# Attention products in fewer groups, other PSUM homes, and a first weight load in halves: a change to a fused linear-attention and feed-forward kernel

## The chip, the cores and the metric

The kernel runs on one core of a Trainium2 chip. The metric is the device time of one execution in microseconds (us): 514.23 us before, the median of three runs (513.65 to 514.88). The engines are TensorE (PE in the rows; PEld is its weight load), VectorE (DVE), ScalarE (ACT), GpSimd (POOL) and SyncE (SP), which here issues all the DMA transfers.

## The reference

```python
def _attn_ref(r, k, v, w, u) -> np.ndarray:      # 4 batches, 8 heads, 768 steps, head size 48
    for t in range(S):
        kt, vt, rt = (k[:, :, t], v[:, :, t], r[:, :, t])
        cur = np.einsum('bhd,bhe->bhde', u[None] * kt, vt)
        y[:, :, t] = np.einsum('bhd,bhde->bhe', rt, state + cur)
        state = w[None, :, :, None] * state + np.einsum('bhd,bhe->bhde', kt, vt)

def _moe_ref(x, w_in, w_out) -> np.ndarray:      # 3072 tokens, 384 -> 2048 -> 384
    h = x @ w_in
    sp = np.maximum(h, 0.0) + np.log1p(np.exp(-np.abs(h)))
    g = h * erf(sp)
    return (g @ w_out).astype(np.float32)
```

The attention's output, laid out as 3072 tokens of 384 features, is the `x` of the feed-forward. The weights `w_in` and `w_out` arrive as 64-bit floats.

## The kernel before, in words

**Attention.** The 768 steps are cut into six spans of 128, so that with four batches there are 24 chunks, numbered `g` = 0 to 23; four chunks (one span, all batches) make one of six blocks of 512 tokens. For a chunk the kernel scales r and k by powers of the decay (`R`, `K`), multiplies them on TensorE (`A`), masks the product and puts the u-term on its diagonal (`Q`, `M`, `P`), multiplies it with v and the state with r (`Y`, tile `y`), and multiplies k with v (`D`, tile `ds`), which VectorE adds to the state `sbd` (`S`). The result y is split into a rounded part and a residue (`X`), tile `x`.

**Feed-forward.** The work is 96 pairs (block, slice of 128 hidden features), numbered `n`. `f1(n)` (token `f`) is nine matmuls into a PSUM tile `h`: three slices of the input, times high part by high part, high by residue and low by high. Nine element-wise steps make the activation of `h`: `a`, `b`, `c`, `d`, `e`, `h` on ScalarE, `z`, `g` and `l` on VectorE. `h` rounds (tile `gh`) and `l` takes the residue (`gl`). `f2(n)` (token `p`) is nine matmuls of `gh`, `gl` with the output weights into three PSUM tiles `acc`.

**Weights.** `F` loads one of eight groups of 768 columns of `w_in` (F00 to F07) or `w_out` (F10 to F17); the steps `C..a` to `C..f` turn the 64-bit words into a 32-bit value and split it in a high and a low part (`wih`, `wil`, `woh`, `wol`). Group 00 serves the first two slices. There are two raw tiles and one tile `wt` for the value in the making.

**Order.** The string `ORDER` lists every step as a token, and each engine executes its instructions in the order in which the tokens stand there; a `+` at a token's end moves it to GpSimd, a `*` to ScalarE. `W2` is two matmuls on a tile of zeros, which produce nothing. What may wait is only the semaphores: an instruction waits for its operands and for its output's buffer, and everything behind it on its engine waits too.

**PSUM.** Of eight banks, three are the `acc` (pool `ps1`), two belong to `psa` and three to `ps3`. Before, the three of `ps3` hold, once the first four chunks are through, only the `h` tiles, in turn; the two of `psa` hold the A, y and ds of all later chunks. An `h` is read by `act_a`, `act_z`, `act_g`, `act_h` and `act_l`, and `act_g` writes its result back into it (lines 443, 449 and 454), so its bank is free only after `act_l`.

Of the kernel before, what the change touches and what calls it, by code (L numbers as in the profile page):

```python
# [706 lines left out]
P51 Q6c f3 c2 c1 d2 e2 Y4 D4 W2 C10e X4a d1 C10f C02a N5 X4b C02b C02c S4a C02d Y5 W2 p0x p0y p0z L7a F11 F03 L7b e1
a3 X5a b3 C02e R7+ C02f+ X5b g1 S4b h1 M60* M61+ A6 g2 z3 l1 C11a c3 d3 h2 e3 P60 C11b C11c C11d P61 f4 C11e a4 D5 Y6
p1 Q7a+ C11f+ b4 S5b g3 l2 X6a C03a f5 p2 K7+ z4 S5a X6b C03b L8a F12 C03c Q7b N7+ C03d Q7c N6+ M70+ M71+ A7 c4 h3 d4
e4 l3 g4 a5 C03e h4 b5 C03f f6 l4 z5 C12a c5 C12b C12c C12d L8b F14 F13 d5 a6 b6 z6 P70 e5 P71 g5 f7 C12e a7 p3 Y7  # L710
C12f+ Q8a b7 c6 z7 h5 d6 l5 e6 X7a c7 d7 e7 Q8b+ Q8c g6 X7b K8+ M80+ M81+ g7 p4 p5 f8 h6 l6 C13a C13b h7 C13c C13d l7
a8 b8 z8 C13e f9 f10 c8 a9 d8 b9 z9 S4d+ C13f+ R8+ e8 C14a F05 g8 C14b C14c p6 c9 a10 d9 h8 C14d l8 p7x p7y p7z A8 e9
C14e b10 O70a O70b F04 g9 O71a h9 f11 C14f+ P80 z10 l9 C05a a11 c10 b11 C05b P81 d10 O72a e10 z11 C05c g10 C05d p8x
p8y f12 D6 D7 p8z O71b L9a L9b F15 O72b L10a p9 c11 a12 d11 h10 l10 e11 g11 C05e C05f b12 z12 h11 l11 f13 p10 f14 p11
C04a c12 a13 d12 b13 e12 C04b C04c C04d F07 z13 g12 C04e c13 h12 l12 d13 S6a K10+ C04f+ a14 e13 g13 b14 z14 h13 l13
S7a f15 f16 C07a c14 p12 Q9a C07b C07c C07d a15 d14 b15 z15 e14 F06 g14 a16 C07e b16 z16 h14 l14 c15 C07f+ d15 e15 g15
S5d p13 f17 p14 C15a h15 c16 a17 d16 e16 b17 C15b l15 C15c C15d g16 F16 L10b z17 S7b p15x C15e h16 l16 p15y f18 f19
p15z c17 O150a d17 S7c+ S5c+ C15f+ S4c+ Y8 Q9b N8 S6b D8 p16x C06a a18 b18 e17 C06b C06c C06d g17 O151a a19 b19 z19
h17 l17 O150b z18 Q9c O152a c19 p16y p16z O152b F17 L11a L11b O230a O151b O231a p17 C06e d19 e19 c18 S8b C06f f20
Q10a+ g19 d18 h19 l19 e18 R10+ S8d+ Q10b+ C16a g18 h18 C16b l18 a20 f21 f22 b20 z20 a21 c20 d20 b21 e20 p18 C16c C16d  # L720
S8a Q11a g20 Q10c z21 a22 C16e h20 l20 b22 z22 c21 d21 c22 d22 e22 N9+ M90+ R9+ C16f+ g22 p19 f23 e21 h22 a23 g21 l22
# [112 lines left out]
```

## Time and profile before

| what | value |
|---|---|
| median of three runs | 514.23 us |
| the profiled execution's own time | 513.87 us |
| its span in the trace | 511.8 us |
| TensorE busy | 496.6 us, 97% |
| VectorE busy | 357.4 us, 70% |
| ScalarE busy | 390.4 us, 76% |
| GpSimd busy | 135.7 us, 27% |
| granted TensorE clock | 0.997 of full |

The span is the time from the first to the last recorded instruction; about 2 us of the execution lie outside it. An engine's busy time is the time in which at least one of its instructions ran. A row of the timeline gives the start in us, the length in us, the engine, the line of the kernel, the operation, the output and inputs by the program's names, and how many like instructions follow each other; matmuls overlap, so what one costs is read from start to start.

### The profile page before, as it was taken

How to read it: one execution, taken by the hardware profiler on the slowest of the kernel's cores; microseconds unless marked ns; L12 is line 12 of the kernel's file. 1: busy time of each engine (PE TensorE's matmuls, PEld its weight loads, DVE VectorE, ACT ScalarE, POOL GpSimd, SP SyncE). 2: the span in 40 equal slices, each digit the busy share in tenths (PEclk: the TensorE clock that was granted, in tenths of full speed). 3: DMA queues.
4: the chain of work that ended last, by engine and by line, in shares of the span. 5: the costliest groups of instructions: out<-in, count | busy, mean ns of one | idle time of the engine just before them, and what ended most of it. 6: DMA issues, size and time to landing. Idle time of an engine off the chain costs nothing.

```text
span 511.8 us, 11055 instructions
## 1 busy us (share of the span) xinstructions
PE 496.6 (97%) x4476; PEld 391.8 (77%) x4476; DVE 357.4 (70%) x642; ACT 390.4 (76%) x712; POOL 135.7 (27%) x135
## 2 busy tenths in 40 slices
PE   8798899999999999999999999999999999999995
PEld 4666677788877777787787787888777878777884
DVE  7999997888879878777755755676746555445542
ACT  2688888999887666776777867777878678878892
POOL 4564564133542044016001610226032100000000
PEclk9999999999999999999999999999999999999998
DMA  7953631754601072301006102214030000100001
GB/s 276 363 195 119 249 125 62 243 176 153 224 12 42 2 260 96 131 20 73 2 1 215 49 1 86 97 36 167 22 131 1 1 2 3 41 22 0 0 1 67
DMA packets 13993, 48.16 MB, mean 94 GB/s; under 512 B 1776, under 2 KB 2160, under 8 KB 13936
## 3 DMA queue, kind: packets, MB, share of 16 engines
q1 hardware_dynamic: 13936, 47.39, 26.4%
q8 instruction: 37, 0.61, 0.5%
q14 instruction: 20, 0.16, 0.1%
HBM read 41.09 MB, written 6.29 MB: 93 GB/s over the span
## 4 chain that ended last, share of the span: by engine, by line
PE 85%; DVE 5%; DMA 4%; ACT 3%; SPq 1%; issue 1%; ACTq 0%
PE acc L471 38%; PE h L411 37%; PE y L330 6%; PE A L301 3%; DMA out_dram<-o 2%; DMA raw<-in_win_dram 1%; PE ds L353 1%; DMA att<-in_att_dram 1%; DVE wt L130 1%; DVE wt L127 1%; DVE am L309 1%; DVE gl L454 1%; ACT s L435 0%; SPq L72 0%; ACT s L422 0%
## 5 line engine op out<-in xcount | busy, mean ns | idle before, releaser
L411 PE MATMUL h<-x,wih 128*128 128x512 f32 x576 | 184.8, 402 | 1.0 <-DVE gl L454 0.9
L411 PEld LDWEIGHTS h<-x,wih 128*128 128x128 f32 x576 | 106.4, 188 | 29.3 <-DVE gl L454 3.2
L471 PE MATMUL acc<-gh,woh 128*128 128x512 f32 x288 | 116.0, 403 | 0.0
L411 PE MATMUL h<-x,wil 128*128 128x512 f32 x288 | 114.3, 397 | 0.0
L471 PE MATMUL acc<-gh,wol 128*128 128x512 f32 x288 | 114.2, 397 | 0.0
L471 PE MATMUL acc<-gl,woh 128*128 128x512 f32 x288 | 114.1, 396 | 0.0
L427 DVE SCALAR_TENSOR_TENSOR s<-s,h 128x512 f32<-128x512 f32 x96 | 65.2, 683 | 46.8 <-ACT s L422 46.2
L454 DVE TENSOR_TENSOR gl<-h,gh 128x512 fp32r<-128x512 f32 x96 | 66.0, 689 | 39.8 <-ACT gh L449 38.3
L443 DVE SCALAR_TENSOR_TENSOR h<-s,h 128x512 f32<-128x512 f32 x96 | 66.0, 691 | 37.9 <-ACT s L439 37.3
L449 ACT CAST gh<-h 128x512 fp32r<-128x512 f32 x96 | 55.8, 582 | 36.1 <-DVE h L443 20.6
L418 ACT ACTIVATE s<-h 128x512 f32<-128x512 f32 x96 | 56.9, 593 | 27.5 <-PE h L411 27.1
L431 ACT ACTIVATE s<-s 128x512 f32<-128x512 f32 x96 | 60.0, 627 | 22.7 <-DVE s L427 22.4
L471 PEld LDWEIGHTS acc<-gh,woh 128*128 128x128 f32 x288 | 54.2, 188 | 14.2 <-issue 0.8
L411 PEld LDWEIGHTS h<-x,wil 128*128 128x128 f32 x288 | 54.3, 188 | 13.3 <-DVE wil L135 0.3
L471 PEld LDWEIGHTS acc<-gh,wol 128*128 128x128 f32 x288 | 54.3, 188 | 13.1
L471 PEld LDWEIGHTS acc<-gl,woh 128*128 128x128 f32 x288 | 54.3, 189 | 12.5
L422 ACT ACTIVATE s<-s 128x512 f32<-128x512 f32 x96 | 60.4, 630 | 1.7
L435 ACT ACTIVATE s<-s 128x512 f32<-128x512 f32 x96 | 60.4, 630 | 1.7
L439 ACT ACTIVATE s<-s 128x512 f32<-128x512 f32 x96 | 60.1, 629 | 1.7
L283 POOL TENSOR_TENSOR am<-idents,q 128x512 f32<-128x512 f32 x25 | 28.5, 1150 | 76.6 <-PE y L330 65.5
L309 DVE COPY_PREDICATED am<-mask,A 64x128 f32<-64x128 uint32 (+2 forms) x108 | 38.3, 389 | 3.0 <-PE A L301 1.9
L222 POOL TENSOR_TENSOR att<-att,wr 112x512 f32<-112x512 f32 x16 | 21.8, 1363 | 42.8 <-DMA att<-in_att_dram 42.8
(89 smaller groups left out, 467.5 us busy)
## 6 DMA issues: line engine op xcount, KB each, us to landing
att<-in_att_dram SPq DMA_DIRECT2D x22, 608.0 KB, 5.9
att<-in_att_dram SPq DMA_DIRECT2D x24, 512.0 KB, 4.0
raw<-in_win_dram SPq DMA_DIRECT2D x8, 768.0 KB, 4.7
raw<-in_wout_dram SPq DMA_DIRECT2D x8, 768.0 KB, 4.6
out_dram<-o SPq DMA_DIRECT2D x18, 256.0 KB, 2.6
part<-o SPq DMA_DIRECT2D x6, 256.0 KB, 4.8
o<-part SPq DMA_DIRECT2D x6, 256.0 KB, 3.0
att<-in_att_dram SPq DMA_DIRECT2D x2, 224.0 KB, 6.6
```

The lines of the kernel that those rows point to most:

```text
L309: nc.vector.copy_predicated(out=o, data=ap[rows, n, :, i], mask=mask[rows, n, None, i].to_broadcast(list(o.shape)).bitcast(U32))
L411: nc.tensor.matmul(out=h, lhsT=w[:, f, q, :], rhs=x[:, xi, q, :], start=k == 0, stop=k == 8)
L418: nc.scalar.activation(out=s1, in_=e["h"], func=AF.Tanh, bias=FB0, scale=FA0)
L422: nc.scalar.activation(out=s1, in_=s1, func=AF.Tanh, bias=FB1, scale=FA1)
L427: nc.vector.scalar_tensor_tensor(out=e["s"], in0=e["s1"], scalar=FG, in1=e["h"], op0=ALU.mult, op1=ALU.add)
L431: nc.scalar.activation(out=s, in_=s, func=AF.Tanh, bias=FB2, scale=FA2)
L435: nc.scalar.activation(out=s, in_=s, func=AF.Square, bias=FB3, scale=FA3)
L439: nc.scalar.activation(out=s, in_=s, func=AF.Square, bias=FB4, scale=FA4)
L443: nc.vector.scalar_tensor_tensor(out=h, in0=ff[n]["s"], scalar=FC, in1=h, op0=ALU.subtract, op1=ALU.mult, reverse0=True)
L449: nc.scalar.copy(out=e["gh"], in_=e["h"])
L454: eng.tensor_tensor(out=e["gl"], in0=e["h"], in1=e["gh"].bitcast(F32), op=ALU.subtract)
L471: nc.tensor.matmul(out=acc[e], lhsT=w[:, f, es], rhs=g, start=first and i == 0, stop=last and i == 2)
```

## The change

It does four things. The tiles y and ds of all chunks from the fourth on take their banks from `ps3`, where the `h` are; only the A stay in `psa`. The step `act_g` writes its result into the SBUF tile `s` instead of back into `h`, and `act_h` and `act_l` read it there. The first group of input weights is loaded and converted in two halves of 384 columns, with tokens `F00`, `C00.` and `F08`, `C08.`, in one raw tile and one `wt`. And the whole order is another one: 1,747 tokens instead of 1,739, some steps on other engines.

```diff
+    halves = {int(x[1]) for x in ORDER.split() if x[0] == "F" and x[2] == "8"}
+
+    def columns(which, g):
+        if which in halves and g in (0, 8):
+            return 0, slice(0, WG // 2) if g == 0 else slice(WG // 2, WG)
+        return g, slice(g * WG, (g + 1) * WG)
 
     def fetch_w(which, g):
-        raws[which, g] = raw = stage.tile([P, WG], I64, tag="raw", name=f"raw{which}{g}")
-        nc.sync.dma_start(out=raw, in_=(wout if which else win)[:, g * WG:(g + 1) * WG])
+        n, s = columns(which, g)
+        if n == g:
+            raws[which, n] = stage.tile([P, WG], I64, tag="raw", name=f"raw{which}{n}")
+        nc.sync.dma_start(out=raws[which, n][:, s.start - n * WG:s.stop - n * WG],
+                          in_=(wout if which else win)[:, s])
...
         s["y"] = y_product(chunks[g], [s["am", 0], s["am", 1]], g % 4, g < 4, f"y{g}", g in direct,
-                           (ps1, f"acc{g % 2}") if g < 4 else (psa, "A"))
+                           (ps1, f"acc{g % 2}") if g < 4 else (ps3, "h"))
...
-    def ds_product(t, first, name):
-        ds = (ps3 if first else psa).tile([PR, NPAIR, D], F32, tag="h" if first else "A", name=name)
+    def ds_product(t, home, name):
+        ds = home[0].tile([PR, NPAIR, D], F32, tag=home[1], name=name)
...
     def act_g(n):
-        h = ff[n]["h"]
-        nc.vector.scalar_tensor_tensor(out=h, in0=ff[n]["s"], scalar=FC, in1=h, op0=ALU.subtract, op1=ALU.mult,
+        s = ff[n]["s"]
+        nc.vector.scalar_tensor_tensor(out=s, in0=s, scalar=FC, in1=ff[n]["h"], op0=ALU.subtract, op1=ALU.mult,
                                        reverse0=True)
...
-        nc.scalar.copy(out=e["gh"], in_=e["h"])
+        nc.scalar.copy(out=e["gh"], in_=e["s"])
...
-        eng.tensor_tensor(out=e["gl"], in0=e["h"], in1=e["gh"].bitcast(F32), op=ALU.subtract)
+        eng.tensor_tensor(out=e["gl"], in0=e["s"], in1=e["gh"].bitcast(F32), op=ALU.subtract)
...
-            st_.setdefault(num, {})["ds"] = ds_product(chunks[num], num < 4, f"ds{num}")
+            st_.setdefault(num, {})["ds"] = ds_product(chunks[num], (ps3, "h"), f"ds{num}")
...
-L0a L0b L1a F00 L2a L2b L1b L3a U0 L3b B0 B0* C00a R2+ R0 K0 A0 G0 V0 R1 K1 F01 G1 C00b P00 P01 C00c Q0 A1 W2 V1 C00d
+L0a F00 L0b L1a L2a U0 L2b L3a F08 L1b L3b B0 B0* C00a B0 K0 R0 R1+ C00b G0 A0 V0 W2 C00c P00 K1 A1 K2+ G1+ Q0 P01 Q2a
```

The order moves products together on TensorE. Chunks 16 and 17 stand in the middle of the program (`y16` and `ds16` are tiles of chunk 16, `A17_0` of chunk 17, `acc48_0`, `acc48_2`, `gh_51` and `gh_53` are the feed-forward's). Before, TensorE's rows there are three trips, the last of them for ds16 alone:

```order
L330 MATMUL y16_3624<-att16_2869,sbd_147 32x128 x12
...
L330 MATMUL y17_3653<-am17_1_3523,att17_3378 32x128 x5
L471 MATMUL acc48_0_3451<-gh_51_3563,woh_96 128x512
...
L301 MATMUL A18_0_3734<-att18_3382 64x128
...
L353 MATMUL ds16_3767<-att16_2869 32x48
```

In the change ds16 and the A of chunk 17 stand behind y16 with no feed-forward matmul between:

```order
L481 MATMUL acc48_2_3539<-gh_53_3644,wol_97 128x512
L340 MATMUL y16_3698<-att16_3189,sbd_147 32x128 x12
...
L363 MATMUL ds16_3728<-att16_3189 32x48
...
L311 MATMUL A17_0_3745<-att17_3357 64x128
...
L311 MATMUL A17_0_3745<-att17_3357 64x64
```

So what were separate stretches of attention products between feed-forward matmuls became one.

The second place is the first activation on VectorE (`s2_0` is the tile `s` of n = 0, `h0` its PSUM tile, `gl_0` the residue). Before:

```order
L427 SCALAR_TENSOR_TENSOR s2_0_621<-s1_0_618,h0_570 128x512
L135 TENSOR_TENSOR wil_95<-wt01_453,wih_94 128x768
...
L443 SCALAR_TENSOR_TENSOR h0_570<-s2_0_621,h0_570 128x512
L427 SCALAR_TENSOR_TENSOR s2_1_671<-s1_1_666,h1_598 128x512
L427 SCALAR_TENSOR_TENSOR s2_2_676<-s1_2_673,h2_625 128x512
L454 TENSOR_TENSOR gl_0_680<-h0_570,gh_0_678 128x512
```

In the change:

```order
L437 SCALAR_TENSOR_TENSOR s2_1_678<-s1_1_635,h1_614 128x512
L273 TENSOR_TENSOR att6_571<-att6_571,ub_90 128x384
L453 SCALAR_TENSOR_TENSOR s2_0_628<-s2_0_628,h0_556 128x512
L135 TENSOR_SCALAR wt01_686<-wt01_686 128x768
L137 SCALAR_TENSOR_TENSOR wt01_686<-raw01_574,wt01_686 128x768
L140 SCALAR_TENSOR_TENSOR wt01_686<-raw01_574,wt01_686 128x768
L464 TENSOR_TENSOR gl_0_695<-s2_0_628,gh_0_689 128x512
```

The residue reads `s2_0` in SBUF where it read `h0` in PSUM, and the conversion of group 01 now stands between `g` and `l` of the first slice, where it stood ahead of `g`.

## Rows read from the trace of the kernel before

**Rows 1.** The page's first part: busy us, share of the span, instructions

```profile
PE 496.6 (97%) x4476; PEld 391.8 (77%) x4476; DVE 357.4 (70%) x642; ACT 390.4 (76%) x712; POOL 135.7 (27%) x135
```

**Rows 2.** Stretches: us; busy PE, PEld, DVE, ACT, POOL (instructions); clock; DMA

```profile
29.38:56.42 27.04, 23.09 (x335) 16.44 (x333) 26.53 (x44) 23.25 (x46) 12.78 (x9) 1.00 0.50 174
56.42:78.29 21.87, 21.87 (x217) 17.48 (x218) 20.41 (x32) 18.78 (x32) 15.53 (x12) 1.00 0.47 162
78.29:400.00 321.71, 321.51 (x2835) 256.01 (x2835) 232.73 (x420) 250.71 (x453) 90.78 (x87) 1.00 0.27 92
400.00:506.00 106.00, 106.00 (x627) 84.62 (x625) 52.05 (x86) 82.81 (x146) 2.04 (x2) 1.00 0.02 9
```

**Rows 3.** TensorE's timeline: two waits at the start, in brackets what ended them

```profile
52.71 0.73 PE L411 MATMUL h<-x,wih 128*128 128x512 f32 x2 [0.79 <-DVE gl L454]
...
56.42 0.86 PE L330 MATMUL y<-att,sbd 112*32 112x128 f32 x24 [0.86 <-DVE am L309]
```

**Rows 4.** TensorE's timeline around two Y in a row

```profile
259.46 0.39 PE L411 MATMUL h<-x,wil 128*128 128x512 f32 x1
259.78 0.86 PE L330 MATMUL y<-att,sbd 112*32 112x128 f32 x24
...
261.33 0.84 PE L330 MATMUL y<-att,sbd 112*32 112x128 f32 x24
...
262.98 0.72 PE L411 MATMUL h<-x,wih 128*128 128x512 f32 x2
263.54 0.39 PE L411 MATMUL h<-x,wil 128*128 128x512 f32 x1
263.77 0.63 PE L411 MATMUL h<-x,wih 128*128 128x512 f32 x2
264.24 0.40 PE L411 MATMUL h<-x,wil 128*128 128x512 f32 x1
```

**Rows 5.** TensorE's timeline: a D behind a Y

```profile
320.00 0.86 PE L330 MATMUL y<-att,sbd 112*32 112x128 f32 x24
...
321.55 0.52 PE L353 MATMUL ds<-att 128*32 128x48 f32 x32
```

**Rows 6.** TensorE's timeline: a lone A and the next big matmul

```profile
240.87 0.90 PE L301 MATMUL A<-att 48*64 48x128 f32 x32
241.70 0.50 PE L471 MATMUL acc<-gh,woh 128*128 128x512 f32 x1
```

**Rows 7.** TensorE's timeline: two early A in a row, and one

```profile
21.33 1.98 PE L301 MATMUL A<-att 48*64 48x128 f32 x64 [1.13 <-DMA att<-in_att_dram]
23.24 0.89 PE L389 MATMUL y<-x,neg 128*128 128x128 f32 x6
...
64.60 1.10 PE L301 MATMUL A<-att 48*64 48x128 f32 x32
65.63 0.74 PE L411 MATMUL h<-x,wih 128*128 128x512 f32 x2
```

**Rows 8.** Timelines of VectorE (two scalings, fourth gl) and TensorE (p3)

```profile
6.41 0.68 DVE L222 TENSOR_TENSOR att<-att,wr 112x512 f32<-112x512 f32 x1
7.02 0.68 DVE L218 TENSOR_TENSOR att<-att,wk 112x512 f32<-112x512 f32 x1
...
63.63 0.68 DVE L454 TENSOR_TENSOR gl<-h,gh 128x512 fp32r<-128x512 f32 x1
...
69.95 0.39 PE L471 MATMUL acc<-gh,woh 128*128 128x512 f32 x1
```

**Rows 9.** Timelines of VectorE and GpSimd around 18 us

```profile
17.75 1.63 DVE L266 TENSOR_TENSOR att<-att 128x384 f32<-128x384 f32 x1
...
17.37 1.59 POOL L218 TENSOR_TENSOR att<-att,wk 112x512 f32<-112x512 f32 x1
```

**Rows 10.** Two operations of VectorE: duration ns min/median/max, first and last start

```profile
L454 DVE TENSOR_TENSOR gl<-h,gh x96: 673/691/693, 39.5 to 502.5; 128x512 fp32r<-128x512 f32 x96
...
L266 DVE TENSOR_TENSOR att<-att x10: 543/555/1632, 17.7 to 380.5; 128x384 f32<-128x384 f32 x10
```

More of the change, by code (lines that the diff above doesn't have):

```diff
@@ L103, in body @@
     raws = {}
-    def fetch_w(which, g):
-        raws[which, g] = raw = stage.tile([P, WG], I64, tag="raw", name=f"raw{which}{g}")
-        nc.sync.dma_start(out=raw, in_=(wout if which else win)[:, g * WG:(g + 1) * WG])
+    halves = {int(x[1]) for x in ORDER.split() if x[0] == "F" and x[2] == "8"}
[3 more added lines that the diff above has]
+        return g, slice(g * WG, (g + 1) * WG)
+    def fetch_w(which, g):
+        n, s = columns(which, g)
[3 more added lines that the diff above has]
+                          in_=(wout if which else win)[:, s])
     bits = {}
     def load_w(part, eng, which, g):
-        words = raws[which, g].bitcast(I32).rearrange("p (n two) -> p n two", two=2)
+        n, s = columns(which, g)
+        own = slice(s.start - n * WG, s.stop - n * WG)
+        words = raws[which, n][:, own].bitcast(I32).rearrange("p (n two) -> p n two", two=2)
         wl, wh = words[:, :, 0], words[:, :, 1]
-        if part == "a":
-            bits[which, g] = stage.tile([P, WG], I32, tag="wt", name=f"wt{which}{g}", bufs=WTB)
-        t = bits[which, g]
+        if part == "a" and n == g:
+            bits[which, n] = stage.tile([P, WG], I32, tag="wt", name=f"wt{which}{n}", bufs=WTB)
+        t = bits[which, n][:, own]
         v = t.bitcast(F32)
@@ L672, in body @@
                 y = y_product(t, am, b, False, f"gy{b}", False, (psa, "A"))
-                ds = ds_product(t, False, f"gds{b}")
+                ds = ds_product(t, (psa, "A"), f"gds{b}")
                 for hh in range(2):
@@ L707 @@
[L707 to L721, printed above, removed]
@@ new lines @@
+P90 l25 O231c L11a O232a L11b f27 f28 P91 K11 R11+ S5d+ M100+ M101* c26 S6d+ d26 A10 e26 a28 g26 O232b a27 b28 z28
+p24z b27 c28 h26 l26 d28 e28 z27 g28 p25 f29 f30 p26 c27 h28 d27 Q11a P100 l28 a29 b29 z29 e27 g27 P101 c29 d29 e29
+h27 g29 S5c+ S8d+ Q11b+ S6c+ Q11c N11+ Y9 Y10 M110+ M111+ S8c+ N9+ l27 X9a a30 b30 X9b z30 X10a c30 d30 e30 D10 A11
+p27 L12a L12b S10b P110 X10b K12 Q12a+ R12+ g30 h30 S10a P111 S7c p28 f31 a31 D9 Y11 b31 h29 S9b S9a l29 L13a X11a
+Q12b+ Q12c M120+ M121* X11b z31 c31 d31 e31 l30 g31 D11 A12 p29 f32 h31 S11a l31 a32 f33 p30 b32 z32 S11b L14a O232c
@@ new lines @@
+P131 Y12 D12 S9c+ N13+ R14+ S10c+ K14+ M140+ M141+ A14 X12a b42 h41 S12a S12b O311c L15a L15b S12d+ K15+ R15+ Q15a+
+X12b Q15b+ N15+ S10d+ l40 f43 f44 p40 z42 P140 P141 l41 a43 b43 z43 c42 d42 e42 g42 c43 d43 a44 h42 l42 e43 b44 Q15c
+g43 z44 p41 f45 h43 c44 l43 p42 Y14 d44 e44 a45 g44 M150+ b45 z45 X14a c45 M151* X14b D14 A15 h44 d45 e45 p43 f46 a46
+L16a L16b P150 S14a P151 l44 S9d+ R16+ K16+ Q16a+ S14b g45 b46 h45 l45 Y15 X15a Y13 X13a X15b X13b Q16b+ S14d+ z46
+Q16c M160 M161+ A16 D13 D15 c46 d46 e46 p44 S13a S13b S13c S15b g46 h46 S15a O312c L17a L19a L19b L17b f47 a47 l46 b47
@@ new lines @@
+z47 f48 f49 p45 c47 d47 a48 b48 e47 z48 g47 c48 d48 h47 a49 b49 l47 z49 e48 c49 d49 e49 p46 f50 p47x p47y p47z Q19a+
+S13d+ R17+ Q19b+ Q17a+ Q17b+ Q17c g48 M170 h48 O470a a50 g49 P160 P161 l48 O471a h49 b50 z50 l49 f51 a51 b51 O470b
+p48x p48y f52 Q19c z51 O472a c50 d50 c51 e50 d51 p48z g50 e51 a52 b52 h50 g51 l50 z52 M171* p49 f53 p50 f54 c52 d52
+e52 g52 h51 a53 h52 l52 b53 z53 l51 a54 c53 b54 d53 e53 f55 a55 p51 g53 b55 h53 z55 c55 l53 z54 c54 d55 d54 e55 e54
+g55 S12c K17 g54 S15d N16 p52 f56 h54 l54 a56 p53 Y16 b56 D16 A17 z56 h55 X16a c56 d56 L18a L18b N17 X16b S16b P170
@@ new lines @@
+S14c K18+ Q18a+ S16d+ R18+ Q18b+ p54 f57 a57 e56 b57 S16a R19 P171 l55 g56 z57 f58 p55 f59 a58 c57 d57 h56 l56 b58 e57
+S16c g57 h57 z58 Q18c l57 c58 d58 a59 b59 z59 e58 c59 M180+ g58 M181 N19 p56 p57 f60 d59 e59 g59 h59 l59 a60 Y17 D17
+X17a b60 h58 M190+ A18 S17a S17b z60 X17b l58 f61 f62 p58 c60 d60 e60 a61 b61 a62 P180 S17c N18+ g60 z61 P181 Y18 c61
+d61 e61 L20a L20b K20+ Q20a+ K19+ Q20b g61 S15c Q20c M191* D18 A19 p59 h60 l60 X18a b62 S18a M200+ M201* z62 S18b X18b
+S17d+ h61 c62 d62 l61 P190 P191 L21a L21b p60 f63 e62 a63 R21+ R20+ g62 Q21a h62 b63 z63 A20 Y19 D19 p61 L22a L22b
@@ L765 @@
+c94 b95 p91 h93 l93 d94 z95 e94 c95 g94 p92 h94 l94 d95 e95 g95 p93 p94 h95 l95 p95x O950a p95y p95z O792b O951a O952a
+O950b O951b O952b
 """
```

90 lines of the change are left out of this document (42 added, 48 removed).

## The prediction

> **What bounds the kernel now.** I read the first part of the page, then a table of stretches, then the timeline of TensorE, and last the timelines of VectorE and GpSimd in the first 80 us. The page says that TensorE is busy for 97% of the span [rows 1]. The table of stretches says where the rest is [rows 2]: from the first `f` at 29.38 us to 56.42 us TensorE is idle for 27.04 − 23.09 = 3.95 us, from 56.42 to 78.29 us not at all, from 78.29 to 400 us for 0.2 us, and from 400 to 506 us not at all. So there are two regimes. Up to about 56 us TensorE waits, while VectorE is busy for 26.53 of 27.04 us [rows 2]: VectorE sets the pace there. The last two of these waits show for what: an `f` for the `gl` that lets its PSUM bank go, a `y` for its masked products [rows 3]. After 56 us only TensorE's own instruction stream counts. A shorter wait elsewhere is worth nothing there; fewer TensorE cycles are worth their whole length.
>
> That stream has a price beside its matmuls. Inside an `f` one matmul starts 0.23 us after the last, a pair 0.47 us. Where a group of attention products stands between, [rows 4] show three small losses: the group starts 0.32 us after the last big matmul (0.09 too much); the second Y, the last of its group, takes 1.65 us to the next matmul where the first, followed by another Y, takes 1.55 (0.10); and the first pair of the next `f` takes 0.56 us (0.09). A trip out to attention and back thus costs about **0.28 us** on top of the products. From a Y to a D there is no such loss: D starts 1.55 us after Y did [rows 5]. For a lone A the rows give 0.83 us to the next big matmul [rows 6]; two early A's back to back take 1.91 us, where a single one of that form takes 1.03 us, so 0.15 us of a lone A is its way out [rows 7].
>
> **The change part by part.**
>
> *Fewer trips.* By the order of instructions I count contiguous stretches of A, Y and D on TensorE. Before there are 41 from the start of the program, 33 of them after Y7; in the change 22, and 16 after the stretch D6 Y7 D7. Of the 17 that go in the steady part, one goes because D6 and D7 moved ahead, which the start term below counts, and one more joins Y's and D's. The other 15 join an A to a Y or a D. The first kind saves the whole 0.28 us, since Y to D costs nothing [rows 5]. The second kind has no row: nowhere before does an A stand beside a Y or a D. Its bounds are 0 saved, if going from A's 64-row, 64-column form to the 32-column form of Y and D costs as much as a trip through the big matmuls, and 0.28 saved, if it costs nothing. The nearest rows are the A's own exit of 0.15 us, paid on leaving A for a different form [rows 7], and the free step between Y and D, which have one form. A step between A and Y is a change of form too, once instead of the two changes that end one trip and begin the next, so I take half: 0.14 saved. The sum is 15 × 0.14 + 0.28 = **−2.4 us**, between −0.3 and −4.5.
>
> The Trainium skill's "TensorEngine Tiling (Array Packing)", section Tiling Modes, says that changing the tiling mode, not merely the tile, drains TensorE. This case's rows agree as far as they go: Y to D is free and the array's full form to Y is not. By that rule the step from A to Y still pays, and the full saving of 4.5 us would not come.
>
> *The start.* The chain of VectorE decides it. I count its instructions from 6.41 us up to the fourth `gl` (token `l3`), which the matmuls `p3` need. A 512-wide one takes 0.61 us from start to start [rows 8]; in the same way I took 0.47 us for a 384-wide and 0.87 us for a 768-wide one. Before there are 90, 51.5 us of work, and `l3` starts at 63.63 us [rows 8], so 5.7 us went into waits. In the change 16 of these are no longer ahead of it (9.1 us: scalings of chunks 1 and 2, three pieces of group 03's conversion, low halves now on GpSimd), 15 others are (8.1 us), and four conversion steps of the first group are 0.4 us shorter, since only half of it is ahead in that place. That is 2.5 us less work. With the same 5.7 us of waits `l3` starts at 61.1 us and ends near 61.8; TensorE, walked through the change's order with row times, comes to `p3` near 62.8 us, against 69.95 us before [rows 8]. But before it has done `f6`, `f7` and D5 by then, 2 × 2.11 + 0.48 = 4.7 us. So the change is 62.8 + 4.7 − 69.95 = −2.4 us ahead there. It gives back about 1.1 us at once: `f6` needs the low half of group 03, which stands behind two `s_add` on VectorE, and `p4` its `gl`. The first `f` itself starts at about the same time, 28 to 29.5 us, since the last copy of x0 stands behind four scalings of chunk 4's product on ScalarE. The split load adds one issue to SP's queue and moves no byte: as many KB stand ahead of the end of chunk 3 as before.
>
> The step `g` now writes SBUF, so `gl` reads two SBUF operands where one was PSUM. In this trace a `gl` never takes more than 0.693 us, while VectorE's `diag_b`, which reads two SBUF operands, takes 0.543 to 1.632 us [rows 10]; the long one overlaps a scaling on GpSimd that is itself long, and ends only after it [rows 9]. So some `gl` will be longer, by up to 1.1 us. In the steady part VectorE is idle for a quarter of the time [rows 2], which hides it; without that cover 66 `gl` at a third of a chance and half of 1.1 us would be 12 us. At the start there is no cover: of about seven `gl` one or two meet GpSimd, +0.5 us. The start in all: −2.4 + 1.1 + 0.5 = **−0.8 us**, between −2.5 and +1.5.
>
> The Trainium skill's "GPSIMD Engine Reference", section Specifications, says that GpSimd's SBUF interfaces are shared with VectorE, with contention when a VectorE instruction has two SBUF inputs. [Rows 9, 10] agree; the rule speaks against this part of the change.
>
> *PSUM homes.* y and ds of later chunks take banks from the three of `h`; an `h` gives its bank back after `g` instead of `gl`, earlier by the cast and `gl` itself. A late bank stops TensorE: that is the 0.79 us in [rows 3]. In the program's bank assignment most new neighbours lie 4 us or more apart. Four are tight: ds10 follows y9 with only Y10 between (1.55 us, for two passes over y of half a microsecond each); h43 follows ds12, and h61 follows ds17, with one A between (0.83 us, for two `s_add`); ds15 follows y13. VectorE takes an instruction when the last one is done, so I put 0.3 us on each: **+1.2 us**, between 0 and 5. The cast `gh` from SBUF costs ScalarE a little and TensorE nothing: ScalarE is idle for 22% of the steady part [rows 2]. The tail is the same: five `p` in a row, then the output.
>
> **The sum** against the profiled execution's own 513.87 us (0.36 below the median of 514.23): −2.4 − 0.8 + 1.2 = −2.0, 511.9; as a median **512.2 us**.
>
> **The rivals.**
> 1. *The step between A and Y is free.* For it: Y to D is. Against it: the exit of A in [rows 7]. Then −4.5 − 0.8 + 0.7 = −4.6: 509.6 us.
> 2. *The step costs a whole trip*, so joining A's saves nothing: −0.3 − 0.8 + 1.2 = +0.1: 514.3 us, no change. For it: the first matmul of a new form starts late on the way in and on the way out [rows 4], and nothing shows that a step between two small forms is cheaper. The Trainium skill's rule on mode switching ("TensorEngine Tiling (Array Packing)", Tiling Modes) names no size, so it leaves this open.
> 3. *The shared banks become the bound* (slower). After each of the 16 later groups the next `f` needs a bank that a y or ds just held, and VectorE, with longer `gl`, is late by 0.3 us each time: +4.8 instead of +1.2, 513.87 + 0.36 − 2.4 − 0.8 + 4.8 = 515.8 us. It decides once the new idle time of TensorE after 80 us passes 3.2 us. For it: the same wait exists before, [rows 3]. Against it: before there is almost none after 56 us, and VectorE has slack.
>
> **How the numbers follow.** A change of 0.2%, 1.0 us, is about what a measurement of this kernel can tell from none. Forecast (510.7 to 513.2) 0.43, rival 1 0.15, rival 2 0.24, rival 3 0.18. So faster 0.58, the same 0.24, slower 0.18. The range reaches into rivals 1 and 3: 508.6 to 515.8 us.
>
> **What would show it.** The changed profile should have some 17 fewer exits from attention after 80 us. A to Y: the start of Y after the start of an A should be near 0.75 us; 0.68 is rival 1, 0.83 and more is rival 2. `l3` should start near 61 us, and TensorE's idle time from the first `f` to 80 us should be 4 to 6 us. After 80 us it should be about 1 us, by releases of y and ds; above 3 us it is rival 3. Some `gl` should take over 1 us. I am wrong if `gl` on VectorE becomes what `p` waits for in the steady part, or if the first `f` comes later than 30.5 us.

## The result, and the profile after

The change is **slower**: 518.10 us median (515.35 to 521.89, 20 executions) against 514.73 us (513.65 to 516.64, 20) of the kernel before on the same chip, a ratio of 1.0061, interval 1.0044 to 1.0078. Forecast were 512.2 us, 508.6 to 515.8. Besides the median the scatter has grown, from 3.0 to 6.5 us. The profiled execution took 516.21 us (span 514.4), so it is one of the better ones of the change; that matters below.

The first part of the page answers to [rows 1]: TensorE is as busy as before, GpSimd has 16 us more.

```profile
PE 497.6 (97%) x4478; PEld 394.5 (77%) x4478; DVE 356.7 (69%) x634; ACT 397.3 (77%) x730; POOL 151.7 (29%) x143
```

The table of stretches of the changed kernel, in the columns of [rows 2] (the third number from the right is the granted clock); the last two rows are a closer look into the stretch from 205 us:

```profile
27.28:56.42 29.14, 27.37 (x351) 19.23 (x354) 28.82 (x46) 25.33 (x52) 16.69 (x11) 1.00 0.55 189
56.42:78.29 21.87, 20.88 (x252) 16.35 (x241) 21.44 (x33) 18.82 (x31) 5.46 (x4) 1.00 0.59 214
78.29:205.00 126.71, 126.45 (x1025) 101.30 (x1024) 100.75 (x166) 108.15 (x194) 44.43 (x37) 1.00 0.37 121
205.00:216.00 11.00, 8.85 (x32) 6.77 (x31) 7.96 (x8) 7.96 (x14) 10.05 (x12) 0.85 0.19 52
216.00:400.00 184.00, 183.59 (x1792) 148.77 (x1792) 121.26 (x234) 137.53 (x252) 56.93 (x53) 1.00 0.20 68
430.00:506.00 76.00, 74.43 (x318) 59.45 (x318) 35.52 (x56) 60.04 (x106) 0.00 (x0) 1.00 0.03 11
...
208.00:211.20 3.20, 1.10 (x5) 0.57 (x3) 2.52 (x4) 2.09 (x4) 3.20 (x4) 1.00 0.36 136
212.00:216.00 4.00, 4.00 (x12) 3.14 (x12) 3.26 (x2) 2.77 (x5) 3.92 (x7) 0.59 0.01 4
```

The reader is to see two places. Between 205 and 216 us TensorE is idle for 11.00 − 8.85 = 2.15 us, and right behind that idle time the granted clock is 0.59, that is partly at the lower of its two levels: 12 matmuls in 4 us where 17 fit at full clock. And from 430 us on 1.6 us are idle. Everywhere else after 78 us TensorE is idle for 0.3 to 0.4 us per stretch; before it was 0.2 us from 78 to 400 us.

TensorE's timeline shows what the two waits are for, and in the middle a group that the new order joins (A, Y and D) beside a lone A:

```profile
208.71 0.40 PE L421 MATMUL h<-x,wil 128*128 128x512 f32 x1
211.26 0.50 PE L481 MATMUL acc<-gh,woh 128*128 128x512 f32 x1 [2.15 <-DVE o L507]
...
351.31 0.40 PE L421 MATMUL h<-x,wil 128*128 128x512 f32 x1
351.63 0.90 PE L311 MATMUL A<-att 48*64 48x128 f32 x32
352.46 0.86 PE L340 MATMUL y<-att,sbd 112*32 112x128 f32 x24
353.14 1.06 PE L340 MATMUL y<-am,att 128*32 128x128 f32 x32
354.02 0.52 PE L363 MATMUL ds<-att 128*32 128x48 f32 x32
354.47 0.50 PE L481 MATMUL acc<-gh,woh 128*128 128x512 f32 x1
...
419.14 0.90 PE L311 MATMUL A<-att 48*64 48x128 f32 x32
419.97 0.50 PE L481 MATMUL acc<-gh,woh 128*128 128x512 f32 x1
...
428.69 1.06 PE L340 MATMUL y<-am,att 128*32 128x128 f32 x32
431.57 0.19 PE L519 MATMUL cnt<-bad,wr 112*1 112x4 f32 x2 [1.82 <-DVE bad L517]
431.69 0.74 PE L421 MATMUL h<-x,wih 128*128 128x512 f32 x2
```

`p32x`, `p32y` and `p32z` are the thirds of `p32`, one for each `acc`. The steps `O312a`, `O312b`, `O312c` empty the third `acc` of n = 31, the last pair of its block: `a` loads the half-done tile, `b` adds, `c` stores; the text calls this the drain. At 211.26 us `p32z` waits for `O312b`, the addition on VectorE that empties its bank. At 431.57 us the count Z0, a one-time check of an input, waits for `bad`. VectorE's timeline says what stands ahead of both:

```profile
206.71 0.69 DVE L437 SCALAR_TENSOR_TENSOR s<-s,h 128x512 f32<-128x512 f32 x1 [0.47 <-ACT s L432]
208.25 0.55 DVE L280 TENSOR_REDUCE q<-att 128x8 f32<-128x384 f32 x1 [0.85 <-POOL att L276]
209.23 1.38 DVE L276 TENSOR_TENSOR att<-att 128x384 f32<-128x384 f32 x1 [0.43 <-POOL att L273]
210.53 0.67 DVE L507 TENSOR_TENSOR o<-o,acc 128x512 f32<-128x512 f32 x1
...
213.15 3.22 DVE L464 TENSOR_TENSOR gl<-s,gh 128x512 fp32r<-128x512 f32 x1 [0.74 <-ACT gh L459]
...
430.34 1.02 DVE L388 TENSOR_TENSOR x<-y,x 128x384 fp32r<-128x384 f32 x2 [0.67 <-ACT x L385]
431.27 0.15 DVE L517 TENSOR_TENSOR bad<-wp,wc 112x4 f32<-112x4 f32 x1
```

`O312b` (210.53) stands behind `Q13c` and `Q14b`, preparation of later chunks, and these wait for GpSimd; `bad` stands behind two X steps that wait for ScalarE. GpSimd's timeline of the first place:

```profile
205.72 1.39 POOL L273 TENSOR_TENSOR att<-att,ub 128x384 f32<-128x384 f32 x1 [12.44 <-DMA att<-in_att_dram]
207.19 1.02 POOL L276 TENSOR_TENSOR att<-att 128x384 f32<-128x384 f32 x1
208.16 1.03 POOL L273 TENSOR_TENSOR att<-att,ub 128x384 f32<-128x384 f32 x1
209.13 2.38 POOL L293 TENSOR_TENSOR am<-idents,q 128x512 f32<-128x512 f32 x2
211.59 1.54 POOL L382 TENSOR_TENSOR sbd<-sbd,wp 48x192 f32<-48x192 f32 x3
213.10 1.00 POOL L236 TENSOR_TENSOR att<-att,wkn 128x384 f32<-128x384 f32 x1
214.06 1.27 POOL L232 TENSOR_TENSOR att<-att,wr 112x512 f32<-112x512 f32 x1
215.30 0.50 POOL L382 TENSOR_TENSOR sbd<-sbd,wp 48x192 f32<-48x192 f32 x1
```

GpSimd had been idle for 12.44 us until chunk 13 landed at 205.72 us. So a transfer's landing sets when TensorE goes on. And the row at 213.15 us is the third thing to see: a `gl` of 3.22 us, the longest of [rows 10] was 0.693. While it runs GpSimd goes from one instruction to the next, in a row whose gaps are 0.1 us at most.

**Where the time went.** I lined up the two profiled executions by the work that TensorE still has to do (an `f` or `p` counted as 2.11 us, A 0.83, Y 1.56, D 0.42). The change is ahead by 1.4 us at `f9`, by 2.7 at `p32x` (205.4 us), behind by 0.7 at `f37` (215.3 us), ahead by 0.3 at `f60` (330 us), behind by 0.2 at Y23 (426 us), by 2.1 at `f79` and by 1.8 at `f95`, the last `f`. So 1.4 came from the start and 1.3 from the stretch up to 205 us, in which TensorE's own trips are shorter; 3.4 were lost in ten microseconds, 0.9 won back up to 330 us, 0.5 lost again, and 1.9 lost at Z0. The span is longer by 2.6 us, so another 0.8 goes behind `f95`. Of this 0.5 us is a place between the first matmuls of `p95`: the last `gl` starts only 0.1 us before `p95x` (505.61 us), where in the kernel before it started at 502.53 us, 1.3 us ahead of it.

```profile
505.51 0.69 DVE L464 TENSOR_TENSOR gl<-s,gh 128x512 fp32r<-128x512 f32 x1 [0.74 <-ACT gh L459]
...
506.26 0.50 PE L481 MATMUL acc<-gl,woh 128*128 128x512 f32 x1 [0.23 <-DVE gl L464]
```

Ten of the 96 `gl` took over 1 us, 8.1 us more in all than before. TensorE waited behind none of these ten, also not behind the one of 3.22 us: `f37` to `f39` start without a wait.

### The profile page after: what moved, and what is told of

The parts are those of the page before. It is cut to its first block, busy times and chain, and to the rows that moved or that the text cites. A ratio compares the mean times of both kernels' runs of the same rounds, so it can differ in the third digit from the quotient of the medians.

```text
span 514.4 us, 11075 instructions
## 1 busy us (share of the span) xinstructions
PE 497.6 (97%) x4478; PEld 394.5 (77%) x4478; DVE 356.7 (69%) x634; ACT 397.3 (77%) x730; POOL 151.7 (29%) x143
## 4 chain that ended last, share of the span: by engine, by line
PE 77%; DVE 10%; DMA 5%; ACT 3%; issue 2%; SPq 1%; POOL 1%; DVEq 0%; ACTq 0%; POOLq 0%
PE acc L481 34%; PE h L421 33%; PE y L340 5%; DMA att<-in_att_dram 4%; PE A L311 3%; DVE wt L140 1%; DMA out_dram<-o 1%; DVE wt L137 1%; PE ds L363 1%; DVE am L319 1%; DVE s L453 1%; DVE gl L464 1%; DVE wt L135 1%; POOL att L273 1%; DVE att L276 1%
## 5 line engine op out<-in xcount | busy, mean ns | idle before, releaser
L421 PEld LDWEIGHTS h<-x,wih 128*128 128x128 f32 x576 | 107.6, 189 | 29.6 <-DVE s L453 1.9
L464 DVE TENSOR_TENSOR gl<-s,gh 128x512 fp32r<-128x512 f32 x96 | 74.1, 773 | 45.2 <-ACT gh L459 44.3
L453 DVE SCALAR_TENSOR_TENSOR s<-s,h 128x512 f32<-128x512 f32 x96 | 65.5, 684 | 57.3 <-ACT s L449 56.8
L437 DVE SCALAR_TENSOR_TENSOR s<-s,h 128x512 f32<-128x512 f32 x96 | 65.3, 684 | 31.7 <-ACT s L432 28.9
L459 ACT CAST gh<-s 128x512 fp32r<-128x512 f32 x96 | 58.6, 613 | 26.4 <-DVE s L453 23.8
L293 POOL TENSOR_TENSOR am<-idents,q 128x512 f32<-128x512 f32 x22 | 25.1, 1152 | 59.2 <-PE y L340 33.9
L228 POOL TENSOR_TENSOR att<-att,wk 112x512 f32<-112x512 f32 x16 | 22.5, 1407 | 46.9 <-DMA att<-in_att_dram 46.9
## 6 DMA issues: line engine op xcount, KB each, us to landing
att<-in_att_dram SPq DMA_DIRECT2D x24, 512.0 KB, 3.9
```

What stands on the lines that cost most here:

```text
L421: nc.tensor.matmul(out=h, lhsT=w[:, f, q, :], rhs=x[:, xi, q, :], start=k == 0, stop=k == 8)
L437: nc.vector.scalar_tensor_tensor(out=e["s"], in0=e["s1"], scalar=FG, in1=e["h"], op0=ALU.mult, op1=ALU.add)
L453: nc.vector.scalar_tensor_tensor(out=s, in0=s, scalar=FC, in1=ff[n]["h"], op0=ALU.subtract, op1=ALU.mult, reverse0=True)
L459: nc.scalar.copy(out=e["gh"], in_=e["s"])
L464: eng.tensor_tensor(out=e["gl"], in0=e["s"], in1=e["gh"].bitcast(F32), op=ALU.subtract)
```

## The experiments

Three theories. **1**: the order; at two places VectorE's queue holds what TensorE waits for behind steps that wait for a transfer or for ScalarE. **2**: the banks that y and ds share with `h`. **3**: `gl`, now with two SBUF operands, is held up by GpSimd. Each ratio is against the kernel before on the same chip (513 to 517 us there, medians 514.9 to 515.4); an interval of a ratio is about ±0.002, ±1 us. The diffs of the order show the tokens around the moved ones, not whole lines.

**Z0 one step later.**

```diff
-X22a X22b X23b Z0 f79 f80
+X22a X22b X23b f79 Z0 f80
```

> The change with one token moved: Z0 stands behind f79 instead of ahead of it. Theory 1 (the loss sits where TensorE waits for an instruction that stands late in VectorE's queue): the wait of 1.82 us of cnt for bad at 431.6 us goes, so 518.1 - 1.8 = 516.3 us, and no row of cnt with a wait of over 0.3 us. Theory 2 (the loss is spread over the PSUM banks that y and ds share with h) and theory 3 (gl with two SBUF operands holds VectorE up): the wait turns up at the next f or p and the time stays within 0.5 us of 518.1.

516.15 us (513.1 to 518.9), 1.0023 [1.0005, 1.0041]: 1.95 less than the change, as theory 1 says, and `cnt` has no wait left. In this profile TensorE doesn't wait for `O312b`, but `f39` for 1.60 us at 216.33 us, for a `g` behind a `gl` of 3.88 us.

**The addition ahead of the preparation**, alone and with Z0:

```diff
-l33 a34 b34 z34 Q13c Q14b p32x p32y f36 a35 b35 O312b z35
+l33 a34 b34 z34 p32x p32y f36 a35 b35 O312b Q13c Q14b z35
```

> The change with two tokens moved: Q13c and Q14b stand behind O312b on VectorE instead of ahead of it. Theory 1: p32z no longer waits 2.15 us for O312b at 211.3 us, and the granted clock does not fall behind it (1.7 us), so 518.1 - 3.85 = 514.25 us; if the clock's fall has nothing to do with the wait, 516.0 us. Theories 2 and 3: the wait goes to another p or f, the time stays within 0.5 us of 518.1.

517.73 us (515.4 to 521.3), 1.0052 [1.0023, 1.0082].

> The change with both moves: Z0 behind f79, and Q13c and Q14b behind O312b. Theory 1: both gains, 518.1 - 1.8 - 3.85 = 512.4 us, 0.995 to 0.997 of the kernel before; TensorE's waits after 80 us add up to under 2.5 us and no single one is over 0.5 us. Theories 2 and 3: the loss stays, 517 to 518 us.

516.02 us (512.5 to 518.2), 1.0023 [1.0001, 1.0045]. So theory 1's forecast was missed here: moving the addition gave 0.1 to 0.4 us instead of 3.85. The profiles tell why. `p32z` still waits (0.59 and 0.46 us), now since `O312b` needs the load of its half-done tile, issued at 206.61 us after an output tile's buffer came free; and `f39` waits for 0.98 us in both. The place stays late, only its last cause changes.

**gl from PSUM where the banks allow it** (53 of 96 n), on top of both moves:

```diff
+        ff[n]["v"] = s if n in IN_SBUF else ff[n]["h"]
-        nc.vector.scalar_tensor_tensor(out=s, in0=s, scalar=FC, in1=ff[n]["h"], op0=ALU.subtract, op1=ALU.mult,
+        nc.vector.scalar_tensor_tensor(out=ff[n]["v"], in0=s, scalar=FC, in1=ff[n]["h"], op0=ALU.subtract, op1=ALU.mult,
```

> As the run with both moves, and for 53 of the 96 n (those whose three banks of h allow it) step g writes back into the PSUM bank of h, and gh and gl read it there, as in the kernel before; 43 n keep SBUF. Theory 1: VectorE's queue hides the longer gl, so no more than 0.7 us either way from the run with both moves. Theory 3: these 53 gl are again at 0.67 us, and the time is 1.5 us or more below the run with both moves. Theory 2: the banks come free later by a cast and a gl for these 53, so the time is 1.5 us or more above it.

541.21 us, 1.0525 [1.0491, 1.0560]. Its list of waits (us in total, times, longest):

```profile
PE h L421 <- DVE gl L465: 15.2, 12, 2.7
PE ds L363 <- DVE gl L465: 3.8, 2, 3.5
PE y L340 <- DVE gl L465: 3.6, 2, 2.7
```

22.6 us of waits for banks that `gl` now gives back. Theory 2 is right in this: in the new order three banks for `h`, y and ds are enough only because `g` writes SBUF. As a test of theory 3 it was of no use, the banks cover it.

**Preparation behind `g36`**, on top of both moves: N12 and R13 out of the way of `f39`.

```diff
-p34 N12 l35 R13 c36 z37 d36 a38 p35 c37 e36 g36 f39
+p34 l35 c36 z37 d36 a38 p35 c37 e36 g36 N12 R13 f39
```

> As the run with both moves, and two more tokens moved: N12 and R13, attention preparation on VectorE, stand behind g36 instead of ahead of l35 and z37. In the profile of the run with both moves f39 waits 0.98 us at 223.29 for a g that stands behind them (N12 takes 2.30 us there beside GpSimd). Theory 1 (VectorE's queue order): that wait goes, no wait of f39 over 0.3 us, and the median falls by about 1.2 us, from 516.0 to 514.8. Theory 3 (GpSimd slows VectorE's two-operand steps wherever they stand): l35 is still above 1.5 us, the wait stays within 0.4 us of 0.98 and the median within 0.5 us of 516.0.

514.21 us (512.0 to 517.0), 0.9996 [0.9976, 1.0017]; `f39` has no wait over 0.15 us. `p32z` waits for 1.57 us for the load. As theory 1 says the wait of `f39` went, and the change is level with the kernel before; the median is 1.8 us lower where 1.2 was expected.

**A third buffer for o**, so that this load is early, on top of that; and the same kernel profiled again.

```diff
+ name=f"o{n}_{e}", bufs=None if n == NS - 1 and e == 2 else 3)
-O310a O311a L14b L13b ... O310c O312a
+O310a O311a O312a L14b L13b ... O310c
```

> As the run with N12 and R13 moved, and a third buffer for the output tiles o, so that the load O312a is issued beside O310a and O311a some 10 us earlier. In the run with both moves p32z still waits 0.46 us at 210.4 for O312b, which by then waits for that load. Theory 1 in the form that what is late on VectorE is late because a load lands late: p32z's wait goes, and the median is 0.5 to 1.0 us below the run without the third buffer, since it also varies less. Rival: another VectorE step ahead of O312b holds it, and both the wait and the time stay.

516.24 us (511.48 to 518.8), 1.0033 [1.0015, 1.0051], though its profile is of the 511.48 us and `p32z` doesn't wait in it. The profile is of the lowest of the twelve, and the median did not follow it.

> The run with the third output buffer once more, for a second profile: its profiled execution took 511.5 us, the lowest of twelve, and the median was 516.2. Theory 1: this one shows a wait of 1 us or more at one of the places that vary, the start, the drain at 168 us or 205 to 225 us, and a fallen clock behind it. Rival: no such wait, but matmuls that take longer or a clock that falls with nothing ahead of it.

The second execution took 517.41 us. Here is `gl` of n = 34 in VectorE's timeline, first the execution of 511.48 us, then that of 517.41 us with TensorE's next wait:

```profile
212.09 0.83 DVE L464 TENSOR_TENSOR gl<-s,gh 128x512 fp32r<-128x512 f32 x1 [0.82 <-ACT gh L459]
213.80 0.69 DVE L453 SCALAR_TENSOR_TENSOR s<-s,h 128x512 f32<-128x512 f32 x1 [0.89 <-ACT s L449]
```

```profile
213.65 3.81 DVE L464 TENSOR_TENSOR gl<-s,gh 128x512 fp32r<-128x512 f32 x1 [0.74 <-ACT gh L459]
217.38 0.67 DVE L453 SCALAR_TENSOR_TENSOR s<-s,h 128x512 f32<-128x512 f32 x1
...
218.11 0.74 PE L421 MATMUL h<-x,wih 128*128 128x512 f32 x2 [2.78 <-DVE s L453]
...
216.50:220.50 4.00, 2.39 (x8) 1.89 (x9) 3.54 (x5) 1.99 (x4) 2.09 (x2) 0.82 0.00 0
```

The same program, the same place: 0.83 us or 3.81 us. The `g` behind it is late, with it the bank for the next `f`, and the clock falls (0.82 in the last row); between `p32x` and `f39` the second execution falls behind the first by 4.8 us. This is theory 3. Of the eleven profiles with this `gl` in SBUF operands five show 3.2 to 3.9 us, six 0.7 to 0.8, and where GpSimd's row of instructions stands tells them apart: the six start at most 0.3 us after the first of its three `sbd` steps (211.59 us in the change's first profile), the five 0.9 to 1.6 us after it.

That this `gl` is all that differs between executions is not shown. The lowest execution with Z0 moved, 513.1 us, has the longest of all (3.88 us); one of 519.78 us with the addition moved has 0.69 us, and waits of 1.24 us at 74 us and 1.11 us at 170 us. Part of the scatter goes with the clock: of the change's twenty executions the four with a granted clock of 0.999 took 515.8 to 516.5 us, the five at 0.992 or less 517.9 to 521.9 us.

> The changed kernel once more, unchanged, for a second profile: its executions lie between 515.4 and 521.9 us, the profiled one at 516.2. Theory 1: the same two waits stand there, p32z for O312b at 209 to 213 us (over 1.5 us) and cnt for bad at 430 to 434 us (1.8 us), and what differs is the length of waits at the same few places: the start up to 75 us, the drains at 168 and 211 us, and the steps on VectorE and GpSimd at 215 to 225 us, by 0.5 to 2 us in all. Rival: a wait of over 1 us at a place where no profile so far has one.

517.47 us. As theory 1 says: `p32z` waits 2.44 us for `O312b`, `cnt` 1.82 us, and besides there are 0.61 us for an `f` behind the long `gl`, 0.68 us for ds18 and 0.58 us for an `f` behind x at 367 us. `gl` of n = 34 takes 3.26 us.

**One half-done tile kept in SBUF**, so that `O312b` needs no load (on top of the moves of N12 and R13):

```diff
+            if (b, e) in part and (b, e) == KEPT:
+                outs[n, e] = part[b, e]
+                return
...
+KEPT = (1, 2)
```

> As the run with N12 and R13 moved, and one of the six half-done output tiles (block 1, third 2) stays in SBUF from n = 15 to n = 31 instead of going to DRAM and back, so that O312b waits for no load. In that earlier run p32z still waits 1.57 us at 210.66 for O312b, which waits 2.54 us for its load. Theory 1 (what TensorE waits for late in a drain is a transfer, whose time differs between executions): that wait goes, 1.6 us in the profile, and the median falls from 514.2 to 512.5 or 513. Rival: the median is set by waits elsewhere that the profiled executions don't show, and stays at 514.

516.04 us (510.85 to 518.2), 1.0020 [0.9998, 1.0043]. The profiled execution is the 510.85: no wait over 0.3 us after 74 us. The median did not follow. Theory 1 alone is not enough: its waits are gone from the profile, and the executions still scatter over 7 us.

**That, and one gl of 96 from PSUM.** For n = 34 alone `g` writes the bank of `h` again:

```diff
+        v = ff[n]["v"] = ff[n]["h"] if n in IN_PSUM else s
-        nc.vector.scalar_tensor_tensor(out=s, in0=s, scalar=FC, in1=ff[n]["h"], op0=ALU.subtract, op1=ALU.mult,
+        nc.vector.scalar_tensor_tensor(out=v, in0=s, scalar=FC, in1=ff[n]["h"], op0=ALU.subtract, op1=ALU.mult,
...
+IN_PSUM = {34}
```

> As the run with the tile kept in SBUF, and for one of the 96 n, n = 34, step g writes back into the PSUM bank of h, and gh and gl read it there, as in the kernel before. In 5 of the 12 profiles so far this one gl takes 3.2 to 3.9 us beside GpSimd instead of 0.7 to 1.8, and a wait of TensorE of 1.6 to 2.8 us, with a fallen clock behind it in two, follows. Theory 3 (gl with two SBUF operands is held up by GpSimd, in some executions and not in others): gl of n = 34 stays at 0.7 us, no wait at 215 to 222 us above 0.5 us but one of about 0.3 us of f37 for its bank, and the median falls by 1.0 to 2.5 us from 516.0, with less scatter. Rival (what differs between executions is transfers and the clock): the median stays within 0.7 us of 516.0.

513.19 us (512.0 to 516.9), 0.9976 [0.9957, 0.9996]: 2.85 us less than with this `gl` in SBUF (on another chip; the two ratios' intervals don't meet). It is the best version found, and the interval lies just below 1: **0.2% faster than the kernel before**, though as the lowest of fourteen versions it may owe a part to chance. Its executions still scatter over 4.9 us, against 3.3 us of the kernel before there. Of VectorE's, TensorE's and GpSimd's timelines:

```profile
212.68 0.69 DVE L465 TENSOR_TENSOR gl<-h,gh 128x512 fp32r<-128x512 f32 x1 [0.71 <-ACT gh L460]
...
213.43 0.73 PE L421 MATMUL h<-x,wih 128*128 128x512 f32 x2 [0.73 <-DVE gl L465]
...
211.75 1.55 POOL L382 TENSOR_TENSOR sbd<-sbd,wp 48x192 f32<-48x192 f32 x3
```

The price is a wait of 0.73 us of `f37` for its bank (0.3 was expected). GpSimd goes through the same row of instructions beside it, and `gl` starts 0.93 us after its first `sbd` step, where from SBUF it was long in five profiles of five; in two of the runs below it starts 1.5 and 2.0 us after that step and takes 0.69 us again.

**The SBUF part alone, in the kernel before** (83 of its 96 n; same edit with 13 n in IN_PSUM).

> The kernel before with one part of the change alone: for 83 of the 96 n (those that the two buffers of s allow) step g writes to SBUF, and gh and gl read it there; homes, order and weights as before. Theory 3: some gl take 1 to 3.8 us, but VectorE has its slack in this order, so the time rises by 0 to 2 us, and the executions scatter over 4 us or more instead of 3. Theory 1 (the order alone): within 0.5 us of the kernel before.

522.73 us (520.6 to 523.7), 1.0146 [1.0124, 1.0168], 7.6 us slower: more than either theory expected. The page has both forms of `gl` side by side (count, busy us, mean ns):

```profile
L455 DVE TENSOR_TENSOR gl<-s,gh 128x512 fp32r<-128x512 f32 x83 | 76.8, 928 | 36.8 <-ACT gh L450 34.9
L455 DVE TENSOR_TENSOR gl<-h,gh 128x512 fp32r<-128x512 f32 x13 | 8.9, 684 | 2.2 <-ACT gh L450 2.0
```

In one execution 928 ns from SBUF, 684 ns from PSUM. In all the `gl` take 19.7 us more than before, and between 56 and 506 us TensorE is idle for 5.0 us more. That `s` is held until `gl`, in two buffers, is part of this run too; but in its trace the step that takes a new `s` (`z`) waits for ScalarE's input alone, 40.4 us in all where it was 46.2 before, and never for a buffer.

**What is left of the sum.** Three runs on how the causes add up: n = 34 alone on the changed kernel, with Z0 moved, and with all moves of tokens but no kept tile.

> The changed kernel with one edit: for n = 34 gl reads PSUM. The waits for O312b (2.15 us) and for the count (1.82 us) stay. Theory 3: in its two profiles this gl took 3.2 us and f39 is no more than 0.6 us late by it, since TensorE was already late by the wait for O312b, so it gains less than in the run with the tile kept: 0.5 to 1.5 us below 518.1. If most of the loss is this one gl, 514.5 to 515.5.

519.41 us (515.8 to 522.7), 1.0073 [1.0046, 1.0100]: no gain, a miss. The profiled execution (522.66 us) shows the drain again, later still:

```profile
209.96 0.55 DVE L280 TENSOR_REDUCE q<-att 128x8 f32<-128x384 f32 x1 [2.91 <-POOL att L276]
210.91 1.38 DVE L276 TENSOR_TENSOR att<-att 128x384 f32<-128x384 f32 x1 [0.40 <-POOL att L273]
212.22 0.68 DVE L508 TENSOR_TENSOR o<-o,acc 128x512 f32<-128x512 f32 x1
...
207.84 1.01 POOL L273 TENSOR_TENSOR att<-att,ub 128x384 f32<-128x384 f32 x1 [14.90 <-DMA att<-in_att_dram]
...
212.90:219.00 6.10, 6.05 (x14) 4.79 (x15) 3.93 (x6) 2.90 (x5) 5.69 (x8) 0.50 0.01 3
```

Chunk 13 landed at 207.84 instead of 205.72 us, `p32z` waited for 4.18 us instead of 2.15, and the clock stood at half, the lower of its two levels, for the next 6 us. Between `p32x` and `f39` this execution lost 7.0 us on the kernel before, with a `gl` of 0.69 us: the drain alone can do it.

> The changed kernel with two edits: gl of n = 34 reads PSUM, and Z0 stands behind f79. If the three causes add up (count 1.9, the one gl 0.5 to 1.5, drain and clock the rest), 514.7 to 515.7 us, equal to the kernel before within 0.2%.

515.44 us (513.3 to 518.3), 1.0019 [0.9998, 1.0039], as expected.

> As the run with gl of n = 34 from PSUM and the tile kept in SBUF, but with the tile going to DRAM and back as in the changed kernel: Z0, Q13c, Q14b, N12 and R13 moved and this gl from PSUM. Theory 1 on transfers: p32z waits up to 1.6 us for O312b again and the median is 0.7 to 1.5 us above 513.2. Rival: once that gl is short the drain has time to spare, and the median stays within 0.5 us of 513.2.

514.94 us (513.2 to 519.1), 1.0001 [0.9980, 1.0021]. Beside it: neither edit 514.21, the kept tile alone 516.04, n = 34 alone 514.94, both 513.19 us. Neither gains alone. A late drain and a held `gl` stand at the same place, 3 us apart, and taking one away may leave TensorE to the other; that is a reading, and no run shows it. Four pairs of versions differ in this one `gl` alone, and only one of them gains: 1.0020 to 0.9976 with the kept tile, but 1.0061 to 1.0073 on the change, 1.0023 to 1.0019 with Z0 moved, 0.9996 to 1.0001 with all tokens moved. So the single steps are not settled, only Z0 (1.95 us on the change, 4.0 us from n = 34 alone to n = 34 with Z0) and the way from the change to the best version (4.9 us).

**The halves of the first weight group**, undone twice:

```diff
-F08 C08a C08b C08c C08d C08e C08f
```

> As the run with both moves, without the halves: the first input-weight group and its six conversion steps are whole, at the place of the first half, and the tokens of the second half are gone. If the halves are worth what the prediction's start term says (four conversion steps shorter by 0.4 us each ahead of the fourth gl), TensorE reaches f9 1.0 to 1.6 us later and the time is 1 to 1.6 us above the run with both moves. Rival: the waits of the start (y4 for the masked state, 0.87 to 2.0 us) take it up, and the time stays within 0.5 us.

514.61 us (510.8 to 519.1), 1.0001 [0.9976, 1.0026], 1.4 less than with them (both moves, 516.02 us).

> As the run with the tile kept in SBUF, without the halves (the first input-weight group whole). If the halves cost something, as the median of the run without them says (514.6 against 516.0 us, though its f9 came 0.6 us later in the profile), this is 1 us below the run with the halves. If that difference was scatter, it is 0.3 to 1 us above it.

516.90 us (513.4 to 520.2), 1.0032 [1.0009, 1.0055], 0.9 more than with them (kept tile, 516.04 us). The signs differ, so what the halves are worth stays open within 1.5 us; in the profiles `f9` comes 0.6 and 1.2 us later without them, in both of which other waits of the start move too.

## Why the prediction was wrong

**The start was right.** −0.8 us was forecast. At `f9` the change is ahead by 1.4 us in its profile; over the thirteen profiles in which the start is unchanged the mean is 0.7 (−1.1 to 1.5). `l3` began at 60.8 us (61 forecast), `p3` at 62.9 (62.8). TensorE's idle time in the start was 2.8 us, less than the 4 to 6 forecast.

**Fewer trips were right.** 16 groups after 80 us instead of 33. From A to Y it takes 0.83 us, the sign that was named for rival 2 (a whole trip): Y starts as late after an A as a lone A's next big matmul, 351.63 to 352.46 and 419.14 to 419.97 us. But what [rows 4] showed on the way in (0.09) and in the first pair of the next `f` (0.09) is saved with each joined group, by these rows 16 × 0.18 = 2.9 us. What came of it is read best in the profile with the fewest waits, that of the kept tile: from `f9` to `f95` it gains 1.8 us on the kernel before, and TensorE waits there for some 0.5 us more, so about 2.3 us by this estimate; 2.4 was forecast. The sign was badly chosen: a step between the small forms is not free, and joining still pays. The Trainium skill's "TensorEngine Tiling (Array Packing)", section Tiling Modes, says that a change of tiling mode drains TensorE; the 0.83 us agree with it.

**Shared banks cost less than forecast.** 1.2 us was forecast; the profile has 0.28 us for ds18 and 0.1 us for `f61`, and D10 after Y9 has none. Rival 3's price was met by other means: TensorE's idle time after 80 us is 4.6 us, above the 3.2 us named, and the shared banks have less than a tenth of it.

**What failed are two steps**, and neither of the two signs that were to show an error came: TensorE does not wait for a `gl` between 80 us and the tail, and the first `f` starts at 27.4 us. The first step: "In the steady part VectorE is idle for a quarter of the time [rows 2], which hides it." A quarter free on average says nothing of the ten microseconds in which GpSimd works with hardly a gap, VectorE drains the last tiles of a block, and three banks of `h` wait for `g`. And the price was mis-sized: "up to 1.1 us" was read from one instruction held beside one of GpSimd [rows 9]; beside a row of them it is 2.5 to 3.2 us. The prediction even worked out what it costs without cover (12 us); the kernel before with this part alone lost 7.6. In the change as it stands the cover held better than that: no long `gl` costs TensorE a wait in the first profile, one costs 0.61 us in the second, and `gl` of n = 34 from PSUM alone gained nothing. The Trainium skill's "GPSIMD Engine Reference", section Specifications, which speaks of contention for two SBUF inputs, was weighed and agreed with, and then thought to be hidden.

The second step, which weighs more in the change as it stands: the sum has no term for what stands ahead of `O312b` and `bad` in VectorE's queue. I walked the new order for TensorE's and VectorE's work in the start, and for the banks of y and ds after it, but not for the other releases that TensorE waits for: the additions that empty an accumulator and the one-time count. The two cost 1.8 us (Z0, shown by its run) and, at `p32z`, waits of 2.14 to 4.18 us, with a fallen clock behind three of the four (seen in four of the five profiles that have `O312b` where the change has it; moving the addition alone only handed the wait on to the next cause, so what the drain costs in the median stays open). "The tail is the same" failed too, by 0.8 us in the first profile.

With Z0 and four preparation steps moved, one tile kept and one `gl` in PSUM the rest of the change gives 513.19 us, 1.9 below the kernel before on that chip: the −2.0 that the sum had. That both agree to the tenth is chance, within an interval of ±1 us, and this version has edits that the sum knew nothing of.

## What to carry over

Slack is read at the place: before a lengthened instruction is called hidden, find the stretch where its engine's neighbours are busiest and see what waits behind it there. When an order is rewritten, list for the waiting engine everything that gives it back a bank or an operand, the rare ones too (a drain, a one-time check), and read what stands ahead of each in its own queue. A scatter that grows with a change is a finding: a second profile of the same kernel showed in one row a hold of 3 us that no median had. But a long instruction found there is a cause of the time only once a run without it is faster, and here one pair of four was.
